# Halving the steps that compute a mirrored value by a fifth product, and moving their multiplication from VectorE to GpSimd

## Chip, cores, metric

One core of one Trainium2 chip. The metric is the device time of the slowest (here the only) core in microseconds (us); lower is better. All runs quoted are of the fast state; the granted clock in the records was 0.985 to 0.992.

## The reference, cut to what matters

A two-dimensional Fourier transform of 8 sequences (3008 x 256), its real part, and then a gated feed-forward layer on all 24,064 rows:

```python
X = np.fft.fft(np.fft.fft(x, axis=1), axis=2).real       # x: (8, 3008, 256)
x = X.reshape(24064, 256)
gate = np.maximum(x @ w_gate, 0.0)                        # w_gate, w_val: (256, 1536)
val = x @ w_val
out = (gate * val) @ w_out                                # w_out: (1536, 256)
```

Because the input is real, rows of the transform come in mirrored pairs that share their products up to a sign. The kernel computes gate and value of one row of a pair and gets those of its mirror with little more.

## The kernel before

There are 288 steps: 8 batches of 3 blocks of 12 columns `f`. A step makes one tile `h` (128 x 2 x 512): half 0 for the rows, half 1 for their mirrors. The work is laid on four engines:

- TensorE (PE): two products into G (gate), two into V (value), a third into G to turn it into the mirror's gate, and eight output products of an earlier block.
- ScalarE (ACT): `gs` and `gm`, the two rectified gates, and copies.
- VectorE (DVE): `h` half 0 = gs * V, and for the mirror's value E = af * nb + V (after V's first product), then E = 2E - V (after the second).
- GpSimd (POOL): `h` half 1 = gm * E. In this kernel it reads E here, never V. It also folds the input of a later batch, one piece per step (17 pieces in each of the first six batches; one piece in three is a pair of operations).

Every sixth step, and each of the first 18, does without E. There PE adds a fifth product to V, which becomes the mirror's value, and VectorE multiplies it with gm.

```python
gp = ctx.enter_context(tc.tile_pool(name="gp", bufs=2, space=SB))
ep = ctx.enter_context(tc.tile_pool(name="ep", bufs=4, space=SB))     # 4 buffers each of gm and of E
...
def split(t):
    return 18 <= t < len(steps) and t % 6 != 5

def mirror_gate(t):                                   # issued in step t+1
    nc.tensor.matmul(e["G"][:, cols], lhsT=wm[0][...], rhs=pqt[b, blk][:, 1, cols], start=False, stop=True, ...)
    e["gm"] = ep.tile([128, 512], F32, tag="gm", name="gm")
    nc.scalar.activation(e["gm"][:, cols], e["G"][:, cols], ACTF.Relu)
...
def even(t):                                          # after V's first product
    e["E"] = ep.tile([128, 512], F32, tag="e", name="E")
    nc.vector.scalar_tensor_tensor(e["E"][:, cols], nbt[b, blk][:, cols], af[:, f:f + 1], e["V"][:, cols], ...)

def mirror_h(t, eng, val):                            # h half 1 = gm * val, columns turned round
    eng.tensor_tensor(free(e["h"][:], ...), e["gm"]..., val..., op=ALU.mult)

def mirror_value(t):
    if split(t):
        nc.vector.scalar_tensor_tensor(e["E"][:, cols], e["E"][:, cols], 2.0, e["V"][:, cols], ...)
        mirror_h(t, nc.gpsimd, e["E"])
    else:
        nc.tensor.matmul(e["V"][:, cols], lhsT=wm[1][...], rhs=pqt[b, blk][:, 1, cols], start=False, stop=True, ...)
        mirror_h(t, nc.vector, e["V"])
...
for t in range(n + NF):                               # cut
    if 0 < t <= n: mirror_gate(t - 1)
    if t < n: gate(t)                                 # G's two products, gs
    if 0 < t <= n:
        if split(t - 1): value(t - 1, 1)              # V's second product, then h half 0 on VectorE
        else: mirror_value(t - 1)
    ...
    if split(t):
        value(t, 0); even(t)                          # V's first product, E
    if t >= NF: out_piece(t - NF, 1)
    if 0 < t <= n and split(t - 1): mirror_value(t - 1)
    while folds and next(folds[0], folds) is folds:   # one fold piece per step, on GpSimd
        folds.pop(0)
```

## Time and profile before

| | before |
|---|---|
| median time | 661.86 us (660.03 to 662.0, 5 runs; the first three, known at the prediction, had the median 660.69) |
| profiled span | 660.6 us |
| busy: PE / DVE / ACT / POOL | 637.0 / 553.3 / 426.7 / 468.8 us |
| GpSimd's mirrored multiplications | 225, 1.227 us each |

The page's busy times, and its chain of work that ended last (shares of the span; a q marks an engine's sequencer, "issue" is time in which an engine waited for nothing that the profile shows):

```profile
PE 637.0 (96%) x4266; PEld 410.1 (62%) x4266; DVE 553.3 (84%) x871; ACT 426.7 (65%) x809; POOL 468.8 (71%) x630
...
PE 81%; POOL 11%; DVE 5%; issue 2%; ACT 1%; POOLq 0%; DVEq 0%
```

PE looks like the bound, and for most of the time it is. How much one product costs must be read from starts, not from busy times. In the timeline of before (start, duration, engine, line, operation, output and inputs) products of 512 columns start 0.21 to 0.22 us apart, while each is listed with 0.38 us:

```profile
300.17 0.38 PE L471 MATMUL G<-pq,wc 128*128 128x512 bf16 x1
...
300.38 0.38 PE L472 MATMUL G<-pq,ws 128*128 128x512 bf16 x1
...
300.60 0.38 PE L495 MATMUL V<-pq,ws 128*128 128x512 bf16 x1
```

The next products overlap the end of the last. So a plain step of 1.95 us is five products of 0.216 us and eight output products of 0.109 us: PE's own work, without a gap.

The stretches with a fold are different. From the same timeline, GpSimd's multiplications (L509) with the largest fold operation (L99), ScalarE's gm and the next step's gs, and PE's mirrored gate; the bracket is the idle time before the instruction and what ended it:

```profile
323.77 1.80 POOL L99 TENSOR_TENSOR xl<-xl,xh 94x765 f32<-94x765 f32 x1
...
325.54 1.26 POOL L509 TENSOR_TENSOR h<-gm,E 128x512 bf16<-128x512 f32 x1
...
326.84 0.57 ACT L486 ACTIVATE gm<-G 128x480 f32<-128x480 f32 x1 [1.42 <-POOL h L509]
327.30 0.59 ACT L473 ACTIVATE gs<-G 128x512 f32<-128x512 f32 x1
...
327.95 0.36 PE L483 MATMUL G<-pq,wm 128*128 128x480 bf16 x1 [0.97 <-ACT gs L473]
```

Read it upward. PE waited 0.97 us for ScalarE's gs; ScalarE, which took an earlier gm first, had waited 1.42 us with that for a free gm buffer; that came free when GpSimd finished a multiplication, which had stood behind a fold operation of 1.80 us. GpSimd itself, once it has waited for the fold's input (1.06 us at 301.67), is without a pause from there to 345 us: it is behind, and four buffers let it be behind only so far.

The stretch view confirms it for the batch (first line: batch 3, with a fold; second line: batch 6, without one; columns are the window, its length, then busy time of PE, PE's weight loads, DVE, ACT and POOL, each with its instructions; last the granted clock, the DMA engines' busy share and GB/s):

```profile
270.40:346.90 76.50, 75.43 (x520) 49.62 (x519) 66.10 (x105) 51.58 (x98) 59.54 (x79) 1.00 0.44 109
499.90:574.80 74.90, 74.90 (x521) 49.70 (x520) 66.06 (x105) 51.29 (x98) 38.32 (x55) 1.00 0.25 69
```

PE's work is the same; the fold adds 21 us to GpSimd and 1.6 us to the time. PE loses 7.7 us to these waits in the kernel before (who waited <- for whom: us in total, times, longest):

```profile
ACT gm L486 <- POOL h L509: 27.4, 32, 1.4
...
PE G L483 <- ACT gs L473: 7.7, 8, 1.1
...
DVE E L503 <- POOL h L509: 3.3, 11, 0.4
```

The Trainium skill, "Perfetto Trace Analysis", section "Optimization Strategy", describes both halves of this: the most-contended engine may change from one regime of a kernel to another, and a bubble that keeps coming back on the engine that should be saturated can mean too few buffers for the next tile. This trace agrees: two regimes, and a bubble of about 1 us in each fold.

### The profile page before, as it was taken

To read this page: it belongs to the slowest core of one execution; us is meant where nothing else is said; L and a number is where in the kernel's file an instruction comes from. 1 tells how busy PE (TensorE), PEld (TensorE's weight loads), DVE (VectorE), ACT (ScalarE), POOL (GpSimd) and SP (SyncE) were. 2 spreads that over 40 slices of the span, in tenths; PEclk is the share of its full clock that TensorE was granted. 3 is DMA by queue.
4 is the path that set the end of the run, shared out by engine and by line. 5 is a ranking of instruction groups with operands and counts; after the bars stand their busy time and mean duration, and the time that the engine had idled before them with its cause. 6 is when DMAs were issued, how large, how long until landed. Compare 5 with 4: busy or idle time off the path is not lost.

```text
span 660.6 us, 12759 instructions
## 1 busy us (share of the span) xinstructions
PE 637.0 (96%) x4266; PEld 410.1 (62%) x4266; DVE 553.3 (84%) x871; ACT 426.7 (65%) x809; POOL 468.8 (71%) x630
## 2 busy tenths in 40 slices
PE   6789999999999999999999999999999999999997
PEld 3424666665666666666666666666656666666665
DVE  9857688888788887989888887988979898899991
ACT  5465676775667766676676766676666766666662
POOL 9639579959975599658995599756996355455451
PEclk9799999999999999999999999999999999999999
DMA  9792472393126721196114922177111241211113
GB/s 252 239 202 51 127 202 78 85 234 104 42 78 142 192 82 49 41 196 190 40 53 106 226 81 69 51 161 221 41 42 49 67 118 39 81 33 43 51 32 94
DMA packets 32294, 70.76 MB, mean 107 GB/s; under 512 B 4475, under 2 KB 21491, under 8 KB 30227
## 3 DMA queue, kind: packets, MB, share of 16 engines
q1 hardware_dynamic: 29892, 58.16, 32.3%
q0 software_dynamic: 2336, 11.80, 9.0%
q8 instruction: 33, 0.54, 0.3%
q14 instruction: 33, 0.26, 0.1%
HBM read 39.77 MB, written 30.96 MB: 107 GB/s over the span
## 4 chain that ended last, share of the span: by engine, by line
PE 81%; POOL 11%; DVE 5%; issue 2%; ACT 1%; POOLq 0%; DVEq 0%
PE po L539 33%; PE V L495 9%; PE V L493 8%; PE G L472 8%; PE G L471 8%; PE G L483 8%; POOL h L509 3%; POOL eo L102 3%; POOL xl L99 2%; PE V L521 2%; PE ps L162 2%; POOL eo L130 2%; DVE E L503 1%; PE psw L261 1%; PE ps L204 1%
## 5 line engine op out<-in xcount | busy, mean ns | idle before, releaser
L509 POOL TENSOR_TENSOR h<-gm,E 128x480 bf16<-128x480 f32 (+1 forms) x225 | 276.0, 1227 | 147.5 <-DVE E L517 128.2
L539 PE MATMUL po<-wo,h 128*128 128x256 bf16 x2304 | 333.5, 272 | 0.0
L539 PEld LDWEIGHTS <-h 128*128 128x128 bf16 x2304 | 222.7, 98 | 88.2 <-issue 3.9
L486 ACT ACTIVATE gm<-G 128x480 f32<-128x480 f32 (+1 forms) x288 | 167.3, 581 | 141.8 <-PE G L483 112.1
L497 DVE TENSOR_TENSOR h<-gs,V 128x512 bf16<-128x512 f32 x288 | 193.9, 686 | 32.6 <-PE V L495 22.0
L503 DVE SCALAR_TENSOR_TENSOR E<-nb,af,V 128x480 f32<-128x480 bf16 (+1 forms) x225 | 163.0, 724 | 16.4 <-PE V L493 10.5
L473 ACT ACTIVATE gs<-G 128x512 f32<-128x512 f32 x288 | 171.5, 595 | 0.8 <-PE G L472 0.8
L517 DVE SCALAR_TENSOR_TENSOR E<-E,V 128x480 f32<-128x480 f32 (+1 forms) x225 | 148.1, 658 | 0.0
L483 PE MATMUL G<-pq,wm 128*128 128x480 bf16 (+1 forms) x288 | 106.6, 370 | 7.8 <-ACT gs L473 7.7
L495 PE MATMUL V<-pq,ws 128*128 128x512 bf16 x288 | 109.0, 378 | 1.1 <-DVE E L503 0.5
L472 PE MATMUL G<-pq,ws 128*128 128x512 bf16 x288 | 109.1, 379 | 0.4 <-DVE pq L209 0.4
L471 PE MATMUL G<-pq,wc 128*128 128x512 bf16 x288 | 109.1, 379 | 0.0
L493 PE MATMUL V<-pq,wc 128*128 128x512 bf16 x288 | 109.1, 379 | 0.0
L542 ACT COPY os<-po 128x512 f32<-128x512 f32 x96 | 56.2, 586 | 58.4 <-PE po L539 58.4
L509 DVE TENSOR_TENSOR h<-gm,V 128x480 bf16<-128x480 f32 (+1 forms) x63 | 41.9, 665 | 39.3 <-ACT gm L486 33.8
L102 POOL TENSOR_TENSOR eo<-xl 94x381 bf16<-94x381 f32 x70 | 69.0, 992 | 0.4
L99 POOL TENSOR_TENSOR xl<-xl,xh 94x765 f32<-94x765 f32 x35 | 63.2, 1806 | 2.7
L495 PEld LDWEIGHTS <-ws 128*128 128x128 bf16 x288 | 28.1, 98 | 33.9
L472 PEld LDWEIGHTS <-ws 128*128 128x128 bf16 x288 | 28.1, 98 | 31.5 <-issue 0.2
L172 ACT CAST t<-ps 96x512 bf16<-96x512 f32 x63 | 36.9, 585 | 6.6 <-PE ps L160 5.4
L493 PEld LDWEIGHTS <-wc 128*128 128x128 bf16 x288 | 28.1, 98 | 14.8 <-issue 7.0
L471 PEld LDWEIGHTS <-wc 128*128 128x128 bf16 x288 | 28.1, 98 | 13.1 <-issue 9.7
(106 smaller groups left out, 346.0 us busy)
## 6 DMA issues: line engine op xcount, KB each, us to landing
out_dram<-os SPq DMA_DIRECT2D x176, 128.0 KB
xl<-in_x_dram SPq DMA_DIRECT2D x7, 1360.0 KB
Td<-t SPq DMA_DIRECT2D x7, 768.0 KB
t<-Td SPq DMA_DIRECT2D x7, 768.0 KB
nb<-Nd SPq DMA_DIRECT2D x24, 128.0 KB
xl<-in_x_dram SPq DMA_DIRECT2D x7, 238.0 KB
xl<-in_x_dram SPq DMA_DIRECT2D x4, 384.0 KB
xh<-in_x_dram SPq DMA_DIRECT2D x4, 384.0 KB
```

Source lines behind the costliest of these rows:

```text
L471: nc.tensor.matmul(e["G"][:], lhsT=wc[0][:, fs], rhs=pq[:, 0, :], start=True, stop=False)
L472: nc.tensor.matmul(e["G"][:], lhsT=ws[0][:, fs], rhs=pq[:, 1, :], start=False, stop=True)
L473: nc.scalar.activation(e["gs"][:], e["G"][:], ACTF.Relu)
L483: nc.tensor.matmul(e["G"][:, cols], lhsT=wm[0][:, f * 128:(f + 1) * 128], rhs=pqt[b, blk][:, 1, cols], start=False, stop=True, skip_group_ ...
L486: nc.scalar.activation(e["gm"][:, cols], e["G"][:, cols], ACTF.Relu)
L493: nc.tensor.matmul(e["V"][:], lhsT=wc[1][:, fs], rhs=pq[:, 0, :], start=True, stop=split(t))
L495: nc.tensor.matmul(e["V"][:], lhsT=ws[1][:, fs], rhs=pq[:, 1, :], start=False, stop=True, skip_group_check=split(t))
L497: nc.vector.tensor_tensor(e["h"][:, 0, :], e["gs"][:], e["V"][:], op=ALU.mult)
L503: nc.vector.scalar_tensor_tensor(e["E"][:, cols], nbt[b, blk][:, cols], af[:, f:f + 1], e["V"][:, cols], op0=ALU.mult, op1=ALU.add)
L509: eng.tensor_tensor(free(e["h"][:], 512 + cols.start + NB - 1, [NB, (cols.stop - cols.start) // NB], [-1, NB]), e["gm"][:, cols].rearrange ...
L517: nc.vector.scalar_tensor_tensor(e["E"][:, cols], e["E"][:, cols], 2.0, e["V"][:, cols], op0=ALU.mult, op1=ALU.subtract)
L539: nc.tensor.matmul(po[:, s % 2, :], lhsT=ht[t - f + ff]["h"][:, sg, g * 128:(g + 1) * 128], rhs=wo[:, ff, :], start=(ff == 0), stop=(ff == ...
```

## The change

The intent: PE is the busiest engine, so drop half of the remaining fifth products (45 after step 18 become 23); and take the mirrored multiplication of the others off VectorE, the second busiest, by letting ScalarE, which has time, copy V to an E buffer from which GpSimd multiplies.

```diff
     def split(t):
-        return 18 <= t < len(steps) and t % 6 != 5
+        return 18 <= t < len(steps) and t % 12 != 11
@@ mirror_value, the branch with the fifth product
-            mirror_h(t, nc.vector, e["V"])
+            if t < 18:
+                mirror_h(t, nc.vector, e["V"])
+            else:
+                e["E"] = ep.tile([128, 512], F32, tag="e", name="E")
+                nc.scalar.copy(e["E"][:, cols], e["V"][:, cols])
+                mirror_h(t, nc.gpsimd, e["E"])
```

## The prediction

> **What bounds the kernel now.** The page has PE busy 96%, DVE 84%, POOL 71%, ACT 65%; the chain of waits is 81% PE. But it differs by stretch. In the timeline a plain step takes 1.95 us, which is PE's own work: five products (mirrored gate included) start 0.216 us apart, eight output products 0.109 us. The 0.38 us printed for one product is latency; this agrees with the Trainium skill, "TensorE: Matmul & The Clock Gate", section "Step-by-step: what each phase is for" (a stream of products costs about N cycles each, 216 ns for N=512). So a fifth product costs 0.21 us, not 0.38.
> In six stretches GpSimd also folds a later batch (21 us of its time in 17 steps of some 34 us). There POOL is continuously busy (timeline, 303.7 to 345 us), the chain passes through it, and PE idles 0.97 us before the mirrored gate at 327.95. A batch with a fold takes 76.2 us (348.9 to 425.1), one without 74.85 (501.9 to 576.8): a fold costs 1.3 us.
>
> **What the change does.** 45 fifth-product steps after step 18 become 23.
> - PE: 22 products fewer, -4.7 us.
> - DVE: 22 more pairs E (0.72 + 0.66), 45 mirrored multiplications fewer (0.665): about zero.
> - ACT: 23 copies, estimated at 0.58 us each from its other copies: +13 us, with slack.
> - POOL: 45 more multiplications of 1.23 us: +55 us, 469 to 524.
>
> **How much is on the critical path.** Outside the folds POOL needs 1.25 us of each 1.95 us step, so there PE's saving counts: some 10 products, -2 us. Inside a fold POOL never waits, and steps 17, 23 and 29 of a batch, which now relieve it, no longer do: 3.7 us per fold. The four buffers each of gm and E limit its lag. E is tighter: E of step t waits for POOL's multiplication of step t-4, and the next V product waits for E, in PE's order. Before, steps without E stretched that ring. Walking POOL's measured durations through the fold at 301 to 340 us with these rules, stalls begin about step 22 instead of 28, and the batch ends 3.5 us later. For the first fold, where steps are 2.16 us, I get 2.2.
> Sum: 2.2 + 5 x 3.5 - 2 = +17.6 us: 678 us. If only the gm ring counted, about +12.
>
> **What should be seen.**
> - POOL 520 to 525 us busy; PE about 632; DVE within 3 us; ACT +13.
> - POOL's multiplications 270 instead of 225, at the same 1.23 us.
> - "DVE E <- POOL h" and "ACT gm <- POOL h" growing from 3.3 and 27 us to tens of us; PE waits before V's second product or the mirrored gate in six clusters of 4 to 5 us.
> - Batches with a fold about 79.5 us; the last two, without one, about 0.6 us shorter than before. POOL's share of the chain above 15%, from 11%.
>
> **What would make it wrong.** If the lag has more room than the two rings give (the fold ends, and PE never feels the last multiplications), the loss shrinks to 1 to 2 us per fold and the time stays within 2%. If POOL's multiplications slow down, or the late fold delays the next batch's load, it is worse. If only PE's work counted, 656.
>
> Predicted: 678 us, 8 in 10 between 668 and 684; faster 0.02, same 0.2, slower 0.78.

## The result, and the profile after

677.61 us median (676.88 to 678.65, 5 runs). The ratio to before is 1.025 (95% interval 1.0231 to 1.0269): slower. The execution profiled was the one of 676.88 us, whose span is 675.1 us. Ratios here and below are the mean time of one kernel's fast runs over the mean of the other's of the same rounds, so not quite the ratio of the medians quoted.

```profile
PE 636.6 (94%) x4244; PEld 408.6 (61%) x4244; DVE 554.6 (82%) x870; ACT 438.3 (65%) x832; POOL 523.3 (78%) x675
...
PE 54%; POOL 22%; DVE 10%; DMA 7%; issue 5%; ACT 1%; POOLq 0%; DVEq 0%
```

No engine is more than 1.3 us busier than before except GpSimd (+54.5 us) and ScalarE (+11.6 us), and neither is near full. What changed is the chain: GpSimd's share went from 11% to 22%, PE's fell from 81% to 54%. (PE's busy time hardly fell although 22 products are gone. Probably a product that nothing follows closely counts with its whole 0.38 us, and there are more of these; this was not counted.) The DMA's new 7% are three of the fold's loads, 15.6 to 16.1 us each. They did not become a bound: for the loads of the last five folds GpSimd waited 4.5 us in after and 6.7 us in before. The groups of the multiplication in before, and of the multiplication and of the step that makes E in after (busy, mean ns of one, then idle time just before them and its main cause):

```profile
L509 POOL TENSOR_TENSOR h<-gm,E 128x480 bf16<-128x480 f32 (+1 forms) x225 | 276.0, 1227 | 147.5 <-DVE E L517 128.2
```

```profile
L509 POOL TENSOR_TENSOR h<-gm,E 128x480 bf16<-128x480 f32 (+1 forms) x270 | 331.3, 1227 | 112.7 <-DVE E L517 86.6
...
L503 DVE SCALAR_TENSOR_TENSOR E<-nb,af,V 128x480 f32<-128x480 bf16 (+1 forms) x247 | 179.2, 725 | 72.3 <-POOL h L509 50.3
```

The multiplication is not slower, there are just 45 more; nor is VectorE's E (725 ns against 724 in before). And the waits are now these, to compare with those of before:

```profile
DVE E L503 <- POOL h L509: 50.3, 65, 2.3
PE V L495 <- DVE E L503: 21.6, 24, 1.2
...
ACT gm L486 <- POOL h L509: 9.7, 19, 1.6
```

with, further down the list, PE's wait before the mirrored gate at 2.2 us instead of 7.7. The stall has moved. In the timeline of after, in the same batch as above:

```profile
332.71 1.81 POOL L99 TENSOR_TENSOR xl<-xl,xh 94x765 f32<-94x765 f32 x1
...
334.48 1.27 POOL L509 TENSOR_TENSOR h<-gm,E 128x512 bf16<-128x512 f32 x1
...
335.78 0.71 DVE L503 SCALAR_TENSOR_TENSOR E<-nb,af,V 128x480 f32<-128x480 bf16 x1 [1.35 <-POOL h L509]
...
336.54 0.38 PE L495 MATMUL V<-pq,ws 128*128 128x512 bf16 x1 [1.19 <-DVE E L503]
```

Again upward: V's second product may not change V before E has read it (0.71 us, starting at 335.78), and E waits for a buffer that GpSimd frees with its multiplication of 334.48. In before, the mirrored gate waited through gm; here it is E, because now every step takes an E buffer.

The same two batches in the stretch view of after:

```profile
278.90:358.20 79.30, 75.52 (x518) 49.35 (x516) 66.56 (x104) 53.16 (x102) 66.79 (x85) 1.00 0.42 106
516.15:590.00 73.85, 73.85 (x518) 49.38 (x515) 66.32 (x104) 52.48 (x102) 45.72 (x61) 1.00 0.25 70
```

Without a fold the batch became 1.0 us shorter, as intended; with one it became 2.8 us longer. All batches, each from the start of its first step's mirrored gate to that of the next batch (us, read from the timelines):

| batch | 0 | 1 | 2 | 3 | 4 | 5 | 6 (no fold) | 7 to the end (no fold) |
|---|---|---|---|---|---|---|---|---|
| before | 77.8 | 78.7 | 76.8 | 76.5 | 76.2 | 76.8 | 74.9 | 85.8 |
| after | 77.3 | 85.0 | 79.4 | 79.3 | 78.8 | 79.1 | 73.9 | 85.1 |

(The fold of batch 0's steps starts late, at step 24, and ends in batch 1, whose row so holds about a fold and a third.)

### The profile page after: what moved, and what is told of

Its sections match the earlier page's. It is cut to its first block, busy times and chain, and to the rows that moved or that the text cites. A ratio compares the mean times of both kernels' runs of the same rounds, so it can differ in the third digit from the quotient of the medians.

```text
span 675.1 us, 12829 instructions
## 1 busy us (share of the span) xinstructions
PE 636.6 (94%) x4244; PEld 408.6 (61%) x4244; DVE 554.6 (82%) x870; ACT 438.3 (65%) x832; POOL 523.3 (78%) x675
## 4 chain that ended last, share of the span: by engine, by line
PE 54%; POOL 22%; DVE 10%; DMA 7%; issue 5%; ACT 1%; POOLq 0%; DVEq 0%
PE po L544 23%; POOL h L509 8%; DMA xh<-in_x_dram,ix 7%; PE V L495 6%; POOL eo L102 6%; PE V L493 6%; PE G L472 5%; PE G L471 5%; PE G L483 5%; POOL xl L99 5%; DVE E L503 4%; DVE h L497 2%; DVE E L517 2%; POOL eo L130 2%; PE psw L261 1%
## 5 line engine op out<-in xcount | busy, mean ns | idle before, releaser
L509 POOL TENSOR_TENSOR h<-gm,E 128x480 bf16<-128x480 f32 (+1 forms) x270 | 331.3, 1227 | 112.7 <-DVE E L517 86.6
L544 PE MATMUL po<-wo,h 128*128 128x256 bf16 x2304 | 337.1, 272 | 0.0
L503 DVE SCALAR_TENSOR_TENSOR E<-nb,af,V 128x480 f32<-128x480 bf16 (+1 forms) x247 | 179.2, 725 | 72.3 <-POOL h L509 50.3
L497 DVE TENSOR_TENSOR h<-gs,V 128x512 bf16<-128x512 f32 x288 | 196.0, 687 | 15.4 <-ACT gm L486 8.5
L517 DVE SCALAR_TENSOR_TENSOR E<-E,V 128x480 f32<-128x480 f32 (+1 forms) x247 | 162.6, 658 | 0.0
L493 PEld LDWEIGHTS <-wc 128*128 128x128 bf16 x288 | 28.1, 98 | 11.1 <-issue 5.1
L483 PEld LDWEIGHTS <-wm 128*128 128x128 bf16 x288 | 28.2, 98 | 7.5 <-issue 4.1
L204 PEld LDWEIGHTS <-t 128*128 128x128 bf16 x192 | 14.4, 97 | 29.4 <-issue 21.0
```

Source lines behind the costliest of these rows:

```text
L483: nc.tensor.matmul(e["G"][:, cols], lhsT=wm[0][:, f * 128:(f + 1) * 128], rhs=pqt[b, blk][:, 1, cols], start=False, stop=True, skip_group_ ...
L493: nc.tensor.matmul(e["V"][:], lhsT=wc[1][:, fs], rhs=pq[:, 0, :], start=True, stop=split(t))
L497: nc.vector.tensor_tensor(e["h"][:, 0, :], e["gs"][:], e["V"][:], op=ALU.mult)
L509: eng.tensor_tensor(free(e["h"][:], 512 + cols.start + NB - 1, [NB, (cols.stop - cols.start) // NB], [-1, NB]), e["gm"][:, cols].rearrange ...
L544: nc.tensor.matmul(po[:, s % 2, :], lhsT=ht[t - f + ff]["h"][:, sg, g * 128:(g + 1) * 128], rhs=wo[:, ff, :], start=(ff == 0), stop=(ff == ...
```

## The experiments

The theory: GpSimd is overloaded only while it folds, and the ring of four E buffers (then that of gm) hands its lag to PE. Rivals: (A) VectorE, which gets 22 more E pairs, is the bound; (B) ScalarE's copies cost; later (C) every GpSimd multiplication costs, wherever it is. All kernels below gave correct results; times are medians, "before" is the kernel before run on the same chip with them. Eight buffers of both did not fit into the memory, so seven were used. The 95% interval of every ratio to before excludes 1.

### Round 1: the two halves alone, and more buffers (before: 662.13 us)

**freq_only**: only the frequency.

```diff
-        return 18 <= t < len(steps) and t % 6 != 5          # kernel before
+        return 18 <= t < len(steps) and t % 12 != 11
```

> Only the first half of the change: one step in 12 has the fifth product, and its mirrored multiplication stays on VectorE. Theory (GpSimd is overloaded in the folds, four E buffers limit its lag): 22 multiplications go to GpSimd instead of 45, two more per fold instead of three, so about half of the loss: 666 to 671 us; GpSimd about 496 us busy. Rival A (VectorE bounds: the pairs E are what costs): VectorE has here more work than in the changed kernel (22 pairs more and 22 multiplications fewer than before, about +16 us busy), so the whole loss or more: 677 us or above. Rival B (ScalarE's copies cost): no copies here, so no loss: 657 us.

```profile
PE 637.0 (95%) x4244; PEld 408.3 (61%) x4244; DVE 570.1 (85%) x893; ACT 426.8 (64%) x809; POOL 495.3 (74%) x652
```

Measured 671.35 us, ratio 1.014 (1.0113 to 1.0166); GpSimd 495.3 us busy. Just above the theory's range, far from both rivals. VectorE is busiest here (570.1 us, against 554.6 in the changed kernel), and yet the loss is little over half: rival A falls. There is no copy, and yet a loss: rival B falls as the only cause.

**route_only**: only the route.

```diff
-        return 18 <= t < len(steps) and t % 12 != 11        # changed kernel
+        return 18 <= t < len(steps) and t % 6 != 5
```

> Only the second half: still one step in 6 with the fifth product, but ScalarE copies it and GpSimd multiplies it. Theory: GpSimd has the same 45 multiplications more as the changed kernel, so the same stalls in the folds, without the saving of 22 products: 677 to 683 us, GpSimd about 524 us busy. Rival A (VectorE): VectorE loses 45 multiplications (about 30 us busy less) and gains nothing, so no loss: 661 us or below. Rival B (ScalarE): 45 copies instead of 23, so about twice the loss: 690 us.

```profile
PE 640.4 (94%) x4266; PEld 410.6 (60%) x4266; DVE 525.9 (77%) x826; ACT 448.5 (66%) x854; POOL 523.2 (77%) x675
```

Measured 680.67 us, ratio 1.0275 (1.0242 to 1.0307). VectorE is relieved by 27 us (525.9 us busy) and the kernel is 2.7% slower; twice as many copies as in the changed kernel (45) cost nothing like twice the loss. What is common to it and the changed kernel is GpSimd's 523 us. The changed kernel is about 3 us faster; its 22 fewer products would explain that (in outside_only ten of them gain 2.6 us), but the two kernels ran in different rounds and the intervals of their ratios overlap.

**after_ring7** and **before_ring7**: seven buffers of E and of gm in the changed kernel and in the one before.

```diff
-    ep = ctx.enter_context(tc.tile_pool(name="ep", bufs=4, space=SB))
+    ep = ctx.enter_context(tc.tile_pool(name="ep", bufs=7, space=SB))
```

> The changed kernel with seven buffers each of E and gm instead of four: GpSimd has the same work and may lag three steps more. Theory: it never lags so far that E or gm waits for it, the stalls of the folds go, also those that the kernel before had: 645 to 653 us, waits of E and gm for GpSimd's multiplication under 5 us together. Rivals A and B: work of VectorE and ScalarE is unchanged, so the time stays at 675 to 678 us.

> The kernel before with seven buffers each of E and gm: the control. Theory: its smaller stalls (about 1.3 us in each of six folds) go: 652 to 656 us; so that the changed kernel with seven buffers is faster than this one by the saved products, 3 to 7 us. Rivals: no change, 661 us.

Measured 650.31 us (ratio 0.9832) and 652.27 us (ratio 0.9856). Three buffers more of two tiles take 27 us off the changed kernel with no instruction removed, and 10 off the kernel before. The stretch view of after_ring7, batch 2 (with a fold), reads

```profile
193.80:267.60 73.80, 73.80 (x517) 49.38 (x515) 66.26 (x104) 52.43 (x102) 66.90 (x85) 1.00 0.44 113
```

GpSimd works 66.9 us as in the changed kernel (66.8), PE has no gap, and the fold costs nothing. Two expectations were missed in part. The waits of E for GpSimd were not under 5 but 13.3 us; only in batch 1, which lasts 79.1 us against 75.8 in the control and holds 5.0 of the 13.3, do they reach PE (which waits 3.1 us for E there, 3.3 in all). And mostly for that reason the changed kernel gains only 2 us over the control, not 3 to 7. Both kernels compared batch by batch from batch 2 to 6 (73.8 to 74.2 against 74.8 to 74.9) show 0.6 to 1.0 us for three products: 0.2 to 0.3 us each.

### Round 2: where, and which ring (before: 662.34 us)

**outside_only** and **infold_only**: the change only in steps without a fold, or only in those with one (`infold`: steps 24 to 41, and 13 to 30 of batches 1 to 5; 27 and 18 of the 45 fifth-product steps).

```diff
-        return 18 <= t < len(steps) and t % 12 != 11        # changed kernel
+        return 18 <= t < len(steps) and t % (6 if infold(t) else 12) != (5 if infold(t) else 11)
@@
-            if t < 18:
+            if t < 18 or infold(t):                         # infold_only: the two cases swapped
```

> The change only in the steps where GpSimd has no fold to do; in the fold steps the kernel before (one step in 6, VectorE). 10 products fewer. Theory: GpSimd has room there, so each converted step keeps its saving, about 0.3 us by the stepwise comparison of the two kernels with seven buffers: 657 to 660 us against 662 of before. If the GpSimd multiplication cost time wherever it is, 27 more of them (of 45) would bring about 27/45 of the loss: 671 us.

> The opposite: the change only in the 18 fifth-product steps that fall into folds (12 of them lose the product, all 18 multiply on GpSimd). Theory: the whole loss is here, and the gain of the other steps is missing: 678 to 683 us, above the changed kernel. If the cost were spread evenly over GpSimd's multiplications, 18/45 of the loss: 668 us.

Measured 659.72 us (ratio 0.9961, 0.9938 to 0.9984) and 682.03 us (1.0292, 1.0267 to 1.0317). 27 of the 45 multiplications moved to GpSimd cost nothing on balance, and the ten dropped products there gain 2.6 us, about 0.3 each. (One batch did grow in the profiled run: batch 1, from 78.7 to 80.0 us, where GpSimd comes out of one fold and soon goes into the next.) The other 18 multiplications cost 20 us, about 1.1 us each, nearly their whole duration of 1.23 us, although 12 products went with them. Rival C falls: not the multiplication costs, but the multiplication on an engine that is already behind.

**after_e7** and **after_gm7**: seven buffers of one tile only, in the changed kernel.

```diff
-                e["E"] = ep.tile([128, 512], F32, tag="e", name="E")            # both places
+                e["E"] = ep.tile([128, 512], F32, tag="e", bufs=7, name="E")
@@ after_gm7 instead
-        e["gm"] = ep.tile([128, 512], F32, tag="gm", name="gm")
+        e["gm"] = ep.tile([128, 512], F32, tag="gm", bufs=7, name="gm")
```

> The changed kernel with seven buffers of E, four of gm. Theory: E's ring is the tighter by about one step, gm's comes next, so only about a quarter to a third of the loss goes: 669 to 675 us, with the waits of gm for GpSimd's multiplication risen above 30 us and those of E under 5. Rival (E's ring is the only one that matters): as with both at seven, 650 us.

> The changed kernel with seven buffers of gm, four of E. Theory: E's ring holds as before, so nothing is won: 675 to 679 us, waits of E for GpSimd's multiplication still about 50 us. Rival (gm's ring is what counts, as in the kernel before): 670 us or below.

Measured 672.71 us (ratio 1.0158) and 679.71 us (ratio 1.0256, the same as the changed kernel's 1.025). More gm buffers do nothing; more E buffers give back 5 of 16 us, and then the waits are

```profile
ACT gm L486 <- POOL h L509: 60.8, 65, 2.2
...
PE G L483 <- ACT gs L473: 21.4, 21, 1.5
```

while PE no longer waits for E (0.2 us). So the two rings are two bounds on the same lag, E's about one step tighter: the program asks for E of step t in step t, and for gm of step t only in step t+1. Widening one hands the stall to the other; only both together removed it. (VectorE's own waits of E for GpSimd, expected under 5 us, were 8.7.)

### Round 3: the peak instead of the sum, and what comes of it (before: 661.13 us)

**after_spread** and **before_spread**: four buffers as before, but from the second fold on two pieces in three steps, so that a fold takes 27 steps. (The first fold can't be stretched: its data are wanted from step 42 on. A form that stretched it as well would deadlock.)

```diff
-        while folds and next(folds[0], folds) is folds:
+        while folds and (t < 48 or t % 3) and next(folds[0], folds) is folds:
```

> The changed kernel, its rings at four, but from the second fold on the fold puts out two pieces in three steps instead of three: the same work of GpSimd, spread over 27 steps instead of 18. Theory (the peak of GpSimd's load counts, not its sum): most of the loss goes, the first fold's and some of the second's stay: 650 to 660 us, GpSimd about 523 us busy as before. If GpSimd's sum counted: 676 to 679 us.

> The kernel before with the same spread fold: its small stalls of about 1.3 us in five folds go: 653 to 657 us.

Measured 654.01 us (ratio 0.9885) and 652.79 us (ratio 0.9873, just below its range). GpSimd does the same work (522.0 and 469.0 us). So 24 of the changed kernel's 677.6 us hung on how densely the fold pieces stand among the multiplications. With this remedy alone the changed kernel is not faster than the kernel before with the same remedy (1 us slower, inside the scatter of the runs); with seven buffers alone it is 2 us faster.

**spread_ring7** and **allsplit_spread_ring7**: the changed kernel with both remedies; and the same with no fifth product after step 18.

```diff
-        return 18 <= t < len(steps) and t % 12 != 11        # spread_ring7 keeps this line
+        return 18 <= t < len(steps)                         # allsplit_spread_ring7
```

> The changed kernel with the spread fold and seven buffers of both. The one stall of about 4 us that was left with seven buffers stood in the second fold; the spread should take it: 644 to 649 us, below the kernel before with seven buffers (652).

> As the last, and no step after 18 has a fifth product. 23 products fewer, at 0.2 to 0.3 us: 639 to 645 us if only TensorE counts. But VectorE then works about 1.95 us in every step, as long as TensorE: if VectorE has no time left to catch up, 645 to 652 us.

Measured 646.65 us (ratio 0.9786, 0.9766 to 0.9805) and 642.0 us (ratio 0.971, 0.9694 to 0.9726). Both are as expected. The last one beats the kernel before by 2.9%, and spread_ring7 by 4.65 us, about 0.2 us for each of 23 more products dropped: the first intent of the change, taken to its end, pays here. How much of the 2.9% is the change's own is not settled, since the kernel before was not run with both remedies; with one of them it took 652.27 or 652.79 us. In both of those its batches 2 to 6 already last 74.8 to 75.1 us, like batch 6 without a fold, so the second remedy would probably bring little. The busy times and chain of allsplit_spread_ring7 are

```profile
PE 619.2 (97%) x4144; PEld 406.6 (64%) x4221; DVE 584.6 (91%) x916; ACT 422.6 (66%) x809; POOL 521.1 (81%) x675
...
PE 85%; DVE 7%; POOL 3%; issue 2%; ACT 1%; DMA 1%; POOLq 0%; DVEq 0%
```

PE bounds again, GpSimd is nearly gone from the chain though it is as busy as in the changed kernel, and VectorE at 91% may be what comes next. (77 of PE's products are missing from this trace: it lists 4221 weight loads.)

## Why the prediction was right

It said 678 us and the time was 677.61. The mechanism was right: GpSimd's lag in the folds, handed to PE by the rings, E's first. That the total came within 0.4 us is in part luck: the forecast rise of 17.6 us was about 2 us too large (15.75 by the medians), and the 660.69 us that it was added to were 1.2 below the later median. Point by point:

- **A fifth product costs 0.21 us of PE, not 0.38.** Right as to the slot. But dropping one saved more, 0.2 to 0.3 us where nothing else stalls (batch 6: 1.0 us for three; outside_only: 2.6 us for ten). One part of the rest can be read in the timeline of before: after a fifth-product step VectorE first does the mirrored multiplication, so E of the next step comes late, and V's second product at 308.74 starts 0.11 us later than the step's rhythm. The prediction's -2 us for the steps outside the folds was therefore somewhat too small: -2.6 us in outside_only. PE's busy time, forecast as 632 us, was 636.6: a miss.
- **VectorE's work unchanged, ScalarE's copies in slack.** Right: +1.3 us busy, and +11.6 us against +13; freq_only and route_only show that neither counts.
- **45 multiplications more on GpSimd at the same 1.23 us.** Right: 270 at 1227 ns, 523.3 us busy against a forecast of 520 to 525.
- **Cost only in the folds.** Right: infold_only +20 us, outside_only -2.6 us.
- **E's ring is tighter than gm's.** Right: after_gm7 nothing, after_e7 about a third, and then gm holds.
- **Stalls beginning about step 22 and 3.5 us per fold.** From one mirrored gate to the next, the first step that is stretched by over 0.2 us in batches 2 to 5, against batch 6 of the same kernel, is step 20 in after (2.26 to 2.8 us, 1.96 in batch 6) and step 26 in before (3.14 to 3.3 us, 2.16 in batch 6): six steps earlier, as forecast. A batch with a fold costs 1.7 us more than batch 6 in before and 5.3 in after (means of batches 2 to 5), 3.6 more; but against before such a batch grew by 2.6, where the prediction had 3.3 (3.5 less the product of step 5). Here the predicted sum was too large by about 3 us over four batches. Batches 0 and 1 together grew by 5.9 us, against 5.7 forecast, and the last two shrank by 1.7, against 1.3. (The profiled runs differ by 14.5 us, the medians by 15.8: so the forecast of +17.6 was 2 to 3 us too large.) What would account for the difference, the larger saving per product and a fold that starts 0.7 us earlier in its batch (in batch 3, 30.5 us after its start, not 31.25), was not tested by a run of its own.
- **The waits.** "DVE E <- POOL h" rose to 50 us as forecast. PE's clusters of waits, forecast as six of 4 to 5 us, were smaller: before V's second product it waited 2.1 us after the first fold, 5.3 in the second and 3.3 to 3.8 in each of the other four. "ACT gm <- POOL h" did not rise from 27 to tens of us: it fell to 9.7. This was inconsistent with the prediction's own argument: where E's ring holds PE first, the mirrored gate comes late too, and gm's buffer is free by then. after_e7, with E's ring opened, shows the 60.8 us.

One stall stays unsettled: with seven buffers only, batch 1 still lasts 79.1 us. There GpSimd, still behind from the first fold, issues the second fold's load itself, at 135.61 us, and then waits 5.87 us for it before it starts; in the control it issues at 133.21 and waits 4.52. The spread fold removed the stall, but no run moved the load alone.

## What to carry to other kernels

Before giving an underused engine more work, look at the stretches where it does two jobs: its average (71% here) says nothing about a stretch where it is already behind and only a ring of buffers hides it. There each added microsecond cost nearly a microsecond of this whole kernel, while elsewhere the same work was free on balance. If an engine lags for a known burst, try to widen all the rings between it and the bound engine, or to spread the burst; here either was worth far more than the instructions saved, also in the kernel before, which each of them made 8 to 10 us faster.

## What the Trainium skill lacked or had wrong

- "TensorE: Matmul & The Clock Gate", section "Back-to-back issue gap": it gives about 131 ns per product for N=512 in a sustained stream of weight load and product, and says that the 216 ns form over-counts there. In this case's stream, where every product has its own weight load, 512 columns start 0.216 us apart and 256 columns 0.109 us. Its section "Step-by-step: what each phase is for" (216 ns) fits.
- "GPSIMD Engine Reference", section "4.1 Engine selection": about 2x slower than VectorE for an elementwise operation of two inputs. Here the same multiplication took 1.227 us on GpSimd and 0.665 us on VectorE (which read one input from V instead of E): 1.85x. The section agrees roughly, but leaves out this: a multiplication moved there cost the kernel nothing on balance outside the folds and 1.1 us inside them.
- "Perfetto Trace Analysis", section "Optimization Strategy", names too few buffers as a cause of bubbles, and is right; it doesn't say that two rings on the same lagging engine hide each other. Seven buffers of one gave 0 or 5 us, of both 27 us.
